# Second MLP products of the next-to-last rows, moved ahead of the last rows' transposes, in a two-layer transformer kernel

## The chip, the core and the metric

The kernel runs on one core of a Trainium2 chip. The metric is the device time of one execution in microseconds (us). A core has a matrix engine (TensorE, in the profile PE for products and PEld for weight loads), a vector engine (VectorE, DVE), an activation engine (ScalarE, ACT), GpSimd (POOL) and a queue engine (SyncE, SP) that issues transfers. PE writes only into PSUM, which has eight banks of 512 float32 per partition; DVE and ACT read sums out of it. Every engine works through its own list of instructions in order, and an instruction may wait on a semaphore that another engine raises.

## The reference

Two identical layers over x of 2048 rows and 512 columns in bfloat16:

```
x = x + A(layernorm(x))     # 32-head attention of width 16, softmax, then @ wo
x = x + B(layernorm(x))     # relu(. @ w1) @ w2, inner width 1792
x = x + A(layernorm(x))
x = x + B(layernorm(x))
```

The layernorm has no learned scale. What matters here is the very end of the second layer: attention's output projection, the residual sum, the norm, and the two MLP products of the last rows.

## The kernel before

The kernel unrolls everything into five instruction lists. A planner written in the kernel decides the order while the program is built: it keeps estimated clocks for the engines, holds groups of PE work in two lists (`urgent` and `work`), and lets `fill_pe`, `fill_v` and `run_dve` place them between the softmax pieces. A group's sum in PSUM is taken out ("evacuated") by a function that `put_evac` (L428) appends to the list `evac`. None of the planner's tables or costs is touched by the change, and up to the end stage the lists of all engines are the same instruction by instruction.

The second layer's rows are cut into chunks. The last two chunks hold one tile of 128 rows each: chunk 5 (the "former rows", tile 14, called `half_tt`) and chunk 6 (the "last rows", tile 15, called `tt`). For a tile of rows the first MLP product has 14 slices `ht[ft]` of 128 inner columns (`NF` = 14), each 4 products with w1; the second product adds up 14 products with w2. In the buffers' names of the order below, two slices lie in one buffer: `ht0` holds slices 0 and 1, `ht5` holds 10 and 11, `ht6` holds 12 and 13. `xx7` holds the rows of both tiles, `w1_0` to `w1_3` and `ktp0_0` onwards hold w1, `wo` the output projection, `ident` an identity matrix: a product with it copies rows into a sum.

After the softmax loop comes an end stage written out by hand (L2491 to L2637), with these steps:

- The last rows' residual and four products with `wo` are summed into bank `banks[0]`, which is bank 0 of the PSUM tile `ps_s1`. The sum misses one product, that of `ot_last`, which DVE still has to normalise (L1308, L1312, L1314).
- `spare_work` (L2534) gives PE other work while it would wait. It takes first whole groups of the planner's lists, here what is left of the former rows' first MLP product (L733 in the profile, evacuated at L1078 by ACT), and then, by `half_part`, the second MLP products of the former rows: a product of the rows with `ident` and then 14 products of 512 columns, all summed into bank 2 of `ps_s1` (`half_bank`). A condition decides whether `half_part` may run: `if urgent or work or held or half_done[0] == NF` returns. `held` is the list of sums that have been computed and not yet taken out.
- The product with `ot_last` completes the sum. DVE takes statistics straight from PSUM (L2574, L803), ACT computes the root (L806, L811), DVE writes the normalised rows `xn` (L821), and ACT copies the sum into `x_t[tt]` (L2579).
- PE transposes `xn` (L2587), and DVE and ACT copy one half each into `xnT` (L2592).
- A loop over `ft` (14 slices and `LOOK` = 3 steps more) computes the last rows' first product and, three steps later, their second, in two halves of 256 columns in two banks. Relu is done by DVE and ACT in turn (L2620, L2618). Both halves begin with a product that puts the residual in, before the loop. At step `LOOK - 1` the rest of the former rows' `half_part` runs. At step 7 the former rows are copied out and stored (L2608).
- ACT and DVE copy the two halves and two queues store them (L2636, L2637).

PE's products of the end stage all stand under L2511, the helper `add`.

Of the kernel before, what the change touches and what calls it, by code (L numbers as in the profile page):

```python
# [26 lines left out]
def kernel(  # L27
# [10 lines left out]
    nc = tc.nc  # L38
# [9 lines left out]
    NF = DFF // P  # L48
# [71 lines left out]
    LAZY = 2  # L120
    HASTE = 12
    LOOK = 3
    NORM_UNITS, DIRECT_UNITS = 10.0, 3.0

    ctx.enter_context(tc.manual_schedule())
    persist = ctx.enter_context(tc.tile_pool(name="persist", bufs=1))
# [299 lines left out]
        return g  # L426

    def put_evac(cost, fn):  # L428
        evac.append((cost, now_pe[0] + PE_TO_DVE, fn, now_bank[0]))

    def left():
# [15 lines left out]
    def start_group(g):  # L447
        (urgent if g in urgent else work).remove(g)
        n = next_bank()
        if n is None:  # L450
            run_dve(0.0, musts)
            n = next_bank(True)
        now_bank[0] = n
        turn[0] += 1
        owner[n] = "filler"
        ready = max(at(g["deps"], "pe"), bank_free[now_bank[0]] + DVE_TO_PE)
        if g["grid"] and not ending[0]:
            n = len(g["grid"]["mms"])
            grid[0] = dict(
                g["grid"], b=bank(), ready=ready, cols=[deque(range(n)) for _ in range(4)],  # L460
                begun=[False] * 4,
            )
            cur.extend((1.0, grid_unit, ready if n == 0 else 0.0, "f") for n in range(n))
            return
        cur.extend(
            (c, fn, ready if n == 0 else 0.0, g["kind"]) for n, (c, fn) in enumerate(g["pieces"])
        )
# [63 lines left out]
        return worst  # L531

    turn = [0]

    def fill_pe(limit, floor=0.0, most=99):

# [1992 lines left out]

    held = []  # L2530

    of_group = [None]

    def spare_work(units):  # L2534

        while units > 0:
            if not cur:
                g = next(
                    (g for q in (urgent, work) for g in q if at(g["deps"], "pe") is not None), None
                )  # L2540
                if g is None:
                    if urgent or work or held or half_done[0] == NF:
                        return units
                    half_part()
                    units -= 1
                    continue
                start_group(g)
                of_group[0] = g["makes"][0][0]
            units -= cur[0][0]
            do_piece()  # L2550
            if not cur:
                if of_group[0] == "h":
                    do_evac()
                else:
                    held.extend(evac)
                    evac.clear()
        return 0
# [4 lines left out]
            add(banks[i], ot[T][:, part(i)], wo[:, T, :], False, False)  # L2562
    ending[0] = True
    bank_no[0] = 0
    held.extend(evac)
    evac.clear()
    spare_work(DIRECT_UNITS)
    for i in rows:
# [7 lines left out]
    ln_root(tag, n_rows)  # L2576
    for i in rows:
        uses(ln_apply(tag, tt + i, i, at_bank(banks[i])), banks[i], "x")
        uses(nc.scalar.copy(out=x_t[tt + i][:], in_=at_bank(banks[i])), banks[i], "x")  # L2579
    spare_work(NORM_UNITS)  # L2580
    for i in rows:
        for n, copy in enumerate((nc.vector.tensor_copy, nc.scalar.copy)):
# [7 lines left out]
                )  # L2590
            of = pt[:, 0 : NDC * P].rearrange("p (c f) -> p c f", c=NDC)[:, cs.start : cs.stop]
            uses(copy(out=xnT[NQS - 1][:, cs.start : cs.stop, part(i)], in_=of), more[n], "xnT")  # L2592
    spare_work(sum(c for c, *_ in cur))
    evac.extend(held)
    held.clear()
    while evac:
# [3 lines left out]
    ending[0], wide[0] = False, True  # L2600

    halves = [(banks[0], slice(0, D // 2)), (banks[1], slice(D // 2, D))]
    for b, cols in halves:
        add(b, ident[:], x_t[tt][:, cols], True, False, "x")
    for ft in range(NF + LOOK):
        if ft == NF // 2:
            for b, x, row in outs:
# [16 lines left out]
            uses(out, b, "h")  # L2624
        while ft == LOOK - 1 and half_done[0] < NF:
            half_part()
        if ft >= LOOK:
            for b, cols in halves:
                add(
                    b, ht[ft - LOOK][:, part(0)], w2[:, ft - LOOK, cols],  # L2630
                    False, ft == NF + LOOK - 1, "h",
                )
# [35 lines left out]
```

## Time and profile before

| | us |
|---|---|
| median of three runs | 1348.62 (1348.41 to 1348.75) |
| the profiled execution | 1350.76 |
| its span, first to last instruction | 1348.8 |
| busy: PE, ACT, DVE, POOL | 1315.8, 1322.1, 1246.1, 830.0 |
| granted TensorE clock | 0.999 |

The span is what the page's times count from, and the 2 us between it and the profiled execution's time lie around it. Busy times are shares of a span that has many stages; the end stage fills its last 18 us, from about 1330. In the rows of the timeline the columns are the start in us, the length in us, the engine, the line, the operation, what it writes and reads, the count that one row merges, and in brackets the idle time ahead of it and what ended it. A row that merges several products runs from the first one's start to the last one's end, and since products overlap, the spacing of starts is what a product costs in a stream.

### The profile page before, as it was taken

Reading aid. Unit: us, or ns where it says so; the run is one execution under the profiler, and the core shown is the slowest. Engines: PE = TensorE matmul, PEld = TensorE weight load, DVE = VectorE, ACT = ScalarE, POOL = GpSimd, SP = SyncE. Lnnn points to the kernel's source line nnn. Section 1 sums busy time; section 2 is a strip of 40 time slices with the busy share of each in tenths; the row PEclk is TensorE's granted clock in tenths of the full one; section 3 lists DMA queues with packets and bytes.
Section 4 is the critical chain, followed back from the end, with each engine's and each line's share of the span. In section 5 each row is a group of like instructions: output and inputs, shape, how many; then the busy total and the mean of one; then the engine's idle time right before and its main releaser. Section 6 shows DMA issues by size and latency. Waiting matters only on the chain.

```text
span 1348.8 us, 48019 instructions
## 1 busy us (share of the span) xinstructions
PE 1315.8 (98%) x20284; PEld 459.8 (34%) x20284; DVE 1246.1 (92%) x2185; ACT 1322.1 (98%) x1416; POOL 830.0 (62%) x1342
## 2 busy tenths in 40 slices
PE   9999999999999999999999999999999999999997
PEld 3322222222222222222222222222344444444665
DVE  8999999999999999989899899999999998899885
ACT  8999999999999999999999999999999999999995
POOL 4358876667666676756556666566556556567441
PEclk9999999999999999999999999999999999999999
DMA  5301012211042110421113100103302421332120
GB/s 141 67 15 24 14 42 53 50 34 34 14 112 57 34 43 19 108 56 37 30 29 94 42 13 6 35 11 77 97 28 41 112 39 47 75 78 62 28 55 19
DMA packets 166823, 66.52 MB, mean 49 GB/s; under 512 B 137776, under 2 KB 161776, under 8 KB 166608
## 3 DMA queue, kind: packets, MB, share of 16 engines
q1 hardware_dynamic: 160080, 57.86, 17.6%
q0 software_dynamic: 5568, 5.15, 2.1%
q8 instruction: 158, 2.59, 0.8%
q10 hardware_dynamic: 960, 0.46, 0.1%
q14 instruction: 57, 0.47, 0.1%
HBM read 38.80 MB, written 4.19 MB: 32 GB/s over the span
## 4 chain that ended last, share of the span: by engine, by line
PE 58%; ACT 32%; DVE 7%; issue 2%; DMA 1%; POOL 0%; ACTq 0%; DVEq 0%; POOLq 0%
PE ps_s L2396 20%; ACT e L2419 16%; PE ps_f L1430 9%; PE ps_o L1430 9%; PE ps_f L473 9%; PE ps_o L473 8%; ACT xx L2419 5%; ACT w L2419 3%; DVE words L1779 2%; ACT vaug L2419 2%; ACT ktl L2419 2%; ACT val L2419 1%; ACT wv L2419 1%; ACT ktp L2419 1%; PE ps_s L2511 1%
## 5 line engine op out<-in xcount | busy, mean ns | idle before, releaser
L2419 ACT ACTIVATE e<-ps_s 128x1024 bf16<-128x1024 f32 (+1 forms) x702 | 780.9, 1203 | 5.2 <-PE ps_s L2396 4.0
L1779 DVE TENSOR_SCALAR words<-ps_s 128x512 int16<-128x512 f32 x833 | 553.4, 683 | 43.0 <-PE ps_s L2396 36.8
L1848 POOL INT64_ADD words<-words x561 | 355.7, 642 | 240.9 <-DVE words L1779 210.3
L2396 PE MATMUL ps_s<-q,ktp 32*128 32x512 bf16 (+2 forms) x4069 | 474.5, 331 | 14.4 <-ACT e L2419 5.0
L2396 PEld LDWEIGHTS <-ktp 32*128 32x128 bf16 x4317 | 151.6, 91 | 457.6 <-issue 451.4
L2419 ACT ACTIVATE xx<-ps_s 128x1024 bf16<-128x1024 f32 x216 | 234.4, 1122 | 0.7 <-PE ps_s L2396 0.5
L2396 PE MATMUL ps_s<-q,ktl 32*128 32x256 bf16 (+2 forms) x1349 | 195.0, 288 | 1.7 <-ACT wkq L2419 0.5
L1430 PEld LDWEIGHTS <-vaug 128*32 128x32 bf16 x4580 | 113.3, 95 | 144.0 <-issue 128.5
L1430 PE MATMUL ps_f<-e,vaug 128*32 128x512 bf16 (+2 forms) x785 | 115.1, 351 | 0.5 <-DVE ht L1080 0.4
L1430 PE MATMUL ps_o<-e,vaug 128*32 128x512 bf16 (+2 forms) x897 | 111.6, 326 | 0.3 <-DVE ht L1080 0.3
L1430 PE MATMUL ps_f<-words,vaug 128*32 128x512 bf16 (+1 forms) x597 | 99.8, 370 | 1.0 <-issue 1.0
L2419 ACT ACTIVATE w<-ps_s 128x1024 bf16<-128x1024 f32 x86 | 93.6, 1117 | 1.3 <-PE ps_s L2396 1.3
L1779 DVE TENSOR_SCALAR xx<-ps_s 128x512 int16<-128x512 f32 x130 | 85.9, 680 | 2.3 <-PE ps_s L2396 1.2
L1848 POOL INT64_ADD xx<-words x103 | 65.7, 640 | 34.4 <-DVE words L1779 21.8
L2419 ACT ACTIVATE vaug<-ps_s 128x1024 bf16<-128x1024 f32 x77 | 84.1, 1135 | 0.3
L473 PE MATMUL ps_f<-w,ht 128*32 128x512 bf16 x1008 | 82.9, 383 | 0.6 <-DVE r L1286 0.6
L1430 PE MATMUL ps_f<-words,vscaled 128*32 128x512 bf16 (+2 forms) x466 | 83.3, 345 | 0.0
L1430 PEld LDWEIGHTS <-val 128*32 128x32 bf16 x2372 | 68.6, 96 | 38.1 <-issue 31.7
L2396 PEld LDWEIGHTS <-ktl 32*128 32x128 bf16 x1349 | 61.6, 92 | 57.4 <-issue 56.0
L1430 PE MATMUL ps_o<-words,vscaled 128*32 128x512 bf16 (+2 forms) x548 | 78.2, 312 | 0.0
L1430 PEld LDWEIGHTS <-vscaled 128*32 128x32 bf16 x1562 | 66.6, 96 | 27.5 <-issue 21.2
L1848 POOL INT64_ADD words<-xx x85 | 52.5, 626 | 31.5 <-DVE xx L1779 27.5
(360 smaller groups left out, 2815.7 us busy)
## 6 DMA issues: line engine op xcount, KB each, us to landing
w<-in_B_w_dram SPq DMA_DIRECT2D x144, 128.0 KB
w<-in_B_w_dram SPq DMA_DIRECT2D x35, 256.0 KB
q<-xn SPq DMA_DIRECT2D x36, 64.0 KB
wv<-in_A_wqkv_dram SPq DMA_DIRECT2D x8, 256.0 KB
away<-xx SPq DMA_DIRECT2D x8, 256.0 KB
xx<-away SPq DMA_DIRECT2D x8, 256.0 KB
out_dram<-xx SPq DMA_DIRECT2D x15, 128.0 KB
xx<-in_A_x_dram SPq DMA_DIRECT2D x14, 128.0 KB
```

The source lines that it names most:

```text
L473: nc.tensor.matmul(G["b"][cols], lhsT[:, cols], rhs, start=not G["begun"][g], stop=not G["cols"][g], tile_position=(0, 32 * g), skip_group ...
L1430: nc.tensor.matmul((ps_f, ps_o)[sg["bank"]][32 * g : 32 * g + 32, 0 : sg["w"]], values[:, 4 * sg["T"] + g, 2 * e : 2 * e + 32], rhs, start ...
L1779: first = nc.vector.tensor_scalar(out=words[which][:, half * QS : (half + 1) * QS], in0=src, scalar1=EXP_BIAS, scalar2=THIRD, op0=ALU.add, ...
L1848: ins = nc.gpsimd.int64_add(of(part).bitcast(I64), of("lin").bitcast(I64), by)
L2396: score = nc.tensor.matmul(b[:, a : a + sg["w"]], kt[32 * g : 32 * g + 32, kc : kc + P], q_home(sg["q"])[32 * g : 32 * g + 32, sg["e"], 0 ...
L2419: ex = nc.scalar.activation(out=eb[:, 0 : place[m]], in_=b[:, 0 : place[m]], func=ACTF.Exp, scale=1.0 / (LOG2E * UNIT),)
L2511: uses(nc.tensor.matmul(out, lhsT, rhs, start=first, stop=last), b, needs=needs)
```

## The change

Four things change, all in the end stage.

1. An evacuation is now marked when it belongs to a first MLP product (`h`): `put_evac` notes it in `h_evacs`. Where the end stage begins, the sums that wait in `evac` were all put into `held`; now those of `h` are taken out at once and only the others are held.
2. `half_part` may run as soon as the slice that it multiplies has been made, whether or not anything is held.
3. The copy of the last rows' sum to `x_t[tt]` by ACT stands behind the copies of `xnT`, and the two residual products of 256 columns move from before the loop into step `LOOK - 1`.
4. `spare_work` in the norm may place 11 units in place of 10, and one unit more behind the transposes. One `half_part` counts as one unit.

```diff
-    NORM_UNITS, DIRECT_UNITS = 10.0, 3.0
+    NORM_UNITS, DIRECT_UNITS, TURN_UNITS = 11.0, 3.0, 1.0
...
     def put_evac(cost, fn):
+        if of_group[0] == "h":
+            h_evacs.append(fn)
         evac.append((cost, now_pe[0] + PE_TO_DVE, fn, now_bank[0]))
...
-                    if urgent or work or held or half_done[0] == NF:
+                    if half_done[0] == NF or ("h", l, j - 1, half_done[0]) not in made:
                         return units
                     half_part()
...
-    held.extend(evac)
+    for e in evac:
+        if e[2] in h_evacs:
+            e[2]()
+        else:
+            held.append(e)
     evac.clear()
     spare_work(DIRECT_UNITS)
...
         uses(ln_apply(tag, tt + i, i, at_bank(banks[i])), banks[i], "x")
-        uses(nc.scalar.copy(out=x_t[tt + i][:], in_=at_bank(banks[i])), banks[i], "x")
     spare_work(NORM_UNITS)
...
             uses(copy(out=xnT[NQS - 1][:, cs.start : cs.stop, part(i)], in_=of), more[n], "xnT")
-    spare_work(sum(c for c, *_ in cur))
+        uses(nc.scalar.copy(out=x_t[tt + i][:], in_=at_bank(banks[i])), banks[i], "x")
+    spare_work(sum(c for c, *_ in cur) + TURN_UNITS)
...
-    for b, cols in halves:
-        add(b, ident[:], x_t[tt][:, cols], True, False, "x")
     for ft in range(NF + LOOK):
...
         while ft == LOOK - 1 and half_done[0] < NF:
             half_part()
+        for b, cols in halves if ft == LOOK - 1 else ():
+            add(b, ident[:], x_t[tt][:, cols], True, False, "x")
```

Behind these lines the changed kernel's line numbers are five or six higher. The order of the instructions shows what moves. On PE, at the product that completes the last rows' sum, the order before:

```order
L2511 LDWEIGHTS ot_last_148 [waits DVE_49]
L2511 MATMUL ps_s1_181<-wo_67,ot_last_148 128x512
L2587 LDWEIGHTS xn0_168 [waits DVE_49]
L2587 MATMUL ps_o_182<-ident_63,xn0_168 128x128
L2587 LDWEIGHTS xn0_168
```

and now:

```order
L2516 LDWEIGHTS ident_63
L2516 MATMUL ps_s1_181<-xx7_80,ident_63 128x512
L2516 LDWEIGHTS ht0_137
L2516 MATMUL ps_s1_181<-w2_72,ht0_137 128x512
L2516 LDWEIGHTS ot_last_148 [waits DVE_49]
L2516 MATMUL ps_s1_181<-wo_67,ot_last_148 128x512
L2516 LDWEIGHTS ht0_137
L2516 MATMUL ps_s1_181<-w2_72,ht0_137 128x512
L2516 LDWEIGHTS ht1_138
L2516 MATMUL ps_s1_181<-w2_72,ht1_138 128x512
```

Two of the former rows' products stand ahead of `ot_last` and eleven (slices 1 to 11, `ht0` to `ht5`) between it and the transposes. All thirteen stood in one block behind the last rows' third w1 slice. Also on PE, from the last transpose to the first product with w1, before:

```order
L2587 LDWEIGHTS xn0_168
L2587 MATMUL ps_s0_180<-ident_63,xn0_168 128x128
L2511 LDWEIGHTS ident_63
L2511 MATMUL ps_s1_181<-xx7_80,ident_63 128x256 [waits Activation_49]
L2511 LDWEIGHTS ident_63
L2511 MATMUL ps_s1_181<-xx7_80,ident_63 128x256
L2511 LDWEIGHTS w1_2_70
L2511 MATMUL ps_o_182<-xnT3_136,w1_2_70 128x128 [waits DVE_49]
```

and now:

```order
L2592 LDWEIGHTS xn0_168
L2592 MATMUL ps_s0_180<-ident_63,xn0_168 128x128
L2516 LDWEIGHTS ht6_143 [waits Activation_49]
L2516 MATMUL ps_s1_181<-w2_72,ht6_143 128x512
L2516 LDWEIGHTS w1_2_70
L2516 MATMUL ps_o_182<-xnT3_136,w1_2_70 128x128 [waits DVE_49]
```

The two residual products, which wait for ACT's copy, have left this place and stand behind the third w1 slice together with the last product of the former rows (slice 13); the product of slice 12 stands here. On ACT, around the norm, before:

```order
L1078 ACTIVATE ht6_143<-ps_s0_180 128x2x128 [waits PE_49]
L806 ACTIVATE va_176<-mv0_174,masks_64 128x1 [waits DVE_49]
L811 ACTIVATE ya_177<-va_176 128x1 [waits Activation_49]
L2579 CAST xx7_80<-ps_s1_181 128x512 [waits DMAHW3_49,DVE_49,Pool_49]
L2592 COPY xnT3_136<-ps_s0_180 128x2x128 [waits PE_49]
L1078 ACTIVATE ht5_142<-ps_f_183 128x2x128 [waits DMASW7_49,DMASW6_49]
```

and now:

```order
L1083 ACTIVATE ht5_142<-ps_f_183 128x2x128 [waits DMASW6_49,DMASW7_49,DVE_49,PE_49]
L1083 ACTIVATE ht6_143<-ps_s0_180 128x2x128 [waits PE_49]
L811 ACTIVATE va_176<-mv0_174,masks_64 128x1 [waits DVE_49]
L816 ACTIVATE ya_177<-va_176 128x1 [waits Activation_49]
L2597 COPY xnT3_136<-ps_s0_180 128x2x128 [waits PE_49]
L2598 CAST xx7_80<-ps_s1_181 128x512 [waits DMAHW3_49,DVE_49,Pool_49]
```

The evacuation of `ht5` stands first instead of last, and the copy of the sum behind that of `xnT`. The lists of DVE, POOL and SP are the same but for one wait: DVE's last copy (L2636, now L2642) waited for PE and ACT and now waits for PE alone.

More of the change, by code (lines that the diff above doesn't have):

```diff
@@ L453, in start_group @@
         now_bank[0] = n
+        of_group[0] = g["makes"][0][0]
         turn[0] += 1
@@ L533 @@
     turn = [0]
+    of_group = [None]
+    h_evacs = []
     def fill_pe(limit, floor=0.0, most=99):
@@ L2530 @@
     held = []
-    of_group = [None]
     def spare_work(units):
@@ L2547, in spare_work @@
                 start_group(g)
-                of_group[0] = g["makes"][0][0]
             units -= cur[0][0]
```

## The prediction

> **What bounds the kernel now.** The change touches the end stage alone, so I read the span first, then the end stage by stretches, then the chain of waits, then the timeline between the chain's pieces. The view by stretches gives length, busy time of PE, PEld, DVE, ACT and POOL, granted clock, share of DMA and GB/s:
>
> ```profile
> core 0: us, PE busy (x) PEld busy (x) DVE busy (x) ACT busy (x) POOL busy (x), PEclk, DMA share, GB/s
> ...
> 1332.60:1335.06 2.46, 0.00 (x0) 0.00 (x0) 1.69 (x3) 0.50 (x2) 0.00 (x0) 1.00 0.00 0
> 1335.06:1336.61 1.55, 1.28 (x19) 1.14 (x20) 0.54 (x2) 1.17 (x4) 0.00 (x0) 1.00 0.00 0
> 1336.61:1339.85 3.24, 3.24 (x19) 1.47 (x17) 0.34 (x2) 0.25 (x1) 0.00 (x0) 1.00 0.00 0
> 1339.85:1345.50 5.65, 5.65 (x73) 5.09 (x71) 1.46 (x5) 2.14 (x7) 0.00 (x0) 1.00 0.07 23
> 1345.50:1348.80 3.30, 0.02 (x1) 0.00 (x0) 0.42 (x1) 0.37 (x1) 0.00 (x0) 1.00 0.14 40
> ```
>
> PE is empty for 2.46 us, the norm. Soon after, it is full for 3.24 us with the block of 15 wide products of the former rows, and then for 5.65 us with the last rows. The chain that ended last says who sets the pace (start, length, what):
>
> ```profile
> 1332.19 0.41 PE ps_s L2511
> ...
> 1332.68 0.71 DVE stats L2574
> ...
> 1334.20 0.82 DVE xn L821
> ...
> 1335.09 0.59 ACT xx L2579
> ...
> 1345.56 0.02 DVEq L2636
> ...
> 1345.63 0.42 DVE xx L2636
> ```
>
> From the product with `ot_last` (1332.19) the chain goes through DVE and ACT to `xn`, then through ACT's copy of the sum, and from there PE's own list sets the time until DVE's last copy. So the block of 15 lies on the path, while the pause ahead of it is a wait for DVE and ACT in which PE could work.
>
> **The change part by part.** The rows from the timeline on which the sum rests:
>
> ```profile
> 1331.48 0.61 PE L733 MATMUL ps_s<-xnT,ktp 128*128 128x128 bf16 x8
> 1331.78 0.35 DVE L1314 SCALAR_TENSOR_TENSOR ot_last<-ps_o,masks,u 128x128 bf16<-128x128 f32 x1
> 1332.12 0.38 ACT L1078 ACTIVATE ht<-ps_s 128x256 bf16<-128x256 f32 x1 [2.22 <-PE ps_s L733]
> 1332.18 0.10 PEld L2511 LDWEIGHTS <-ot_last 128*128 128x128 bf16 x1 [0.27 <-DVE ot_last L1314]
> ...
> 1335.06 0.28 PE L2587 MATMUL ps_o<-ident,xn 128*128 128x128 bf16 x2 [2.48 <-DVE xn L821]
> ...
> 1335.19 0.28 PE L2587 MATMUL ps_s<-ident,xn 128*128 128x128 bf16 x2
> ...
> 1335.39 0.29 DVE L2592 COPY xnT<-ps_o 128x256 bf16<-128x256 bf16 x1 [0.38 <-PE ps_o L2587]
> 1335.57 0.38 ACT L2592 COPY xnT<-ps_s 128x256 bf16<-128x256 bf16 x1
> 1335.72 0.38 PE L2511 MATMUL ps_s<-xx,ident 128*128 128x256 bf16 x2 [0.26 <-ACT xx L2579]
> ...
> 1335.83 0.40 ACT L1078 ACTIVATE ht<-ps_f 128x256 bf16<-128x256 f32 x1
> 1335.94 0.39 PE L2511 MATMUL ps_o<-xnT,w 128*128 128x128 bf16 x4
> 1336.16 0.61 PE L2511 MATMUL ps_s<-xnT,w 128*128 128x128 bf16 x8
> 1336.36 0.29 DVE L2620 TENSOR_SCALAR ht<-ps_o 128x128 bf16<-128x128 f32 x1 [0.68 <-PE ps_o L2511]
> ...
> 1336.61 0.38 PE L2511 MATMUL ps_s<-xx,ident 128*128 128x512 bf16 x1
> ...
> 1339.85 0.39 PE L2511 MATMUL ps_s<-xnT,w 128*128 128x128 bf16 x4
> ...
> 1340.07 0.38 PE L2511 MATMUL ps_s<-w,ht 128*128 128x256 bf16 x2
> ```
>
> Prices of a product in a stream: the 15 wide ones run from 1336.61 to 1339.85, 3.24/15 = 0.216 us each. The twelve products with w1 run from 1335.94 to 1336.61, 0.67/12 = 0.056 each. The two of 256 columns run from 1335.72 to 1335.94, 0.11 each.
>
> (a) *Two products ahead of `ot_last`: -0.17.* The last of the eight L733 products ends at 1332.09 and, being 0.22 long without its followers, starts at 1331.87; PE is free at 1331.93. Two wide products fill it until 1331.93 + 0.43 = 1332.36, and `ot_last`, ready at 1332.18, starts there and not at 1332.19. Of 0.43 us 0.26 lies in the wait for DVE, and 0.17 delays the norm. Behind `ot_last` wait DVE's statistics and all of the chain. Bounds: 0 (the records put PE free too late) and 0.43 (nothing of it is hidden); I take 0.17, since the wait of 0.27 is in the row.
>
> (b) *Eleven products in the norm: free.* They start at 1332.36 + 0.22 = 1332.58 and take 11 x 0.216 = 2.38, until 1334.96. The norm's length, 1335.06 - 1332.19 = 2.87, is DVE and ACT work that none of these products feeds or delays, since they add into another bank; the transposes come at 1335.06 + 0.17 = 1335.23, and PE is free 0.27 before. Without this cover they would cost their 2.38. The norm could stretch because DVE reads PSUM while PE writes it: I take 0, as DVE's relu reads sums in 0.29 at 1340.71 too, in the stretch where PE is busy 5.65 of 5.65, and 0.1 as the upper end. The last two of the eleven wait for ACT's evacuation of `ht5`, whose sum was complete before the eight L733 products ended; ACT is idle 2.22 us ahead of 1332.12, so 0.40 us of it is done by about 1332.1, `ht6` follows, and va, not due before 1333.6, finds ACT free.
>
> (c) *Behind the transposes: 0.12 more.* Let T be the first transpose. Before, the w1 products began at T + 0.88, because two residual products waited for ACT's copy of the sum; the third of the twelve began at T + 0.99. Now the product of slice 12 runs from T + 0.24 to T + 0.46 while DVE copies `xnT` (done at T + 0.62), so it is hidden. The first w1 product can start at T + 0.67. The third needs ACT's half of `xnT`: ACT took that copy 0.10 after the transposes' end (1335.47), DVE took its own 0.05 after (1335.34 to 1335.39); with the copy of the sum gone from ahead of it, I put ACT at T + 0.45, done at T + 0.83, and the third product at T + 0.88. That is 0.11 to 0.12 earlier. Bounds: 0 (ACT comes no sooner) to 0.3 (no wait for ACT at all).
>
> (d) *The block shrinks from 15 to one.* Ten products from the third w1 on end at T + 0.88 + 0.56 = T + 1.44, the product of slice 13 at T + 1.65, the two residual ones (ACT's copy is over by about T + 1.3) at T + 1.87, the four of the next w1 slice at T + 2.09. There the first product of the last rows starts; before it was 1340.07 = T + 5.01. Its slice was evacuated within 0.32 of its sum's end (1336.33 to 1336.65), that is by T + 1.5 now. Gain 2.92, which is 13 x 0.216 = 2.81 plus the 0.12 of (c).
>
> (e) *The end: 0.05.* DVE's last copy waited with one instruction for PE and with itself for ACT, now for PE only. The extra step in the chain is the 0.02 at 1345.56 with an issue gap: 0.07 from there to 1345.63. I take 0.05, between 0 and 0.07; DVE's half is stored last (SP, below), so it counts.
>
> ```profile
> 1345.91 0.36 ACTq L2637 DMA_DIRECT2D out_dram<-xx  x1
> 1346.08 0.34 SPq L2637 DMA_DIRECT2D out_dram<-xx  x1
> ```
>
> The sum: 2.92 - 0.17 + 0.05 = **2.80 us**. The span goes from 1348.8 to 1346.0 and the profiled execution from 1350.76 to about 1347.96. The three timed runs have a median 2.14 below that execution, and work in the last 18 us moves them alike: 1348.62 - 2.80 = **1345.8 us**, 0.21% less.
>
> One page of the Trainium skill speaks against this size. "TensorE: Matmul & The Clock Gate", section "Back-to-back issue gap", gives 131 ns per product of 512 columns in a stream beside 216 ns for one alone. By 131 ns the thirteen products would be worth 13 x 0.131 = 1.70, and the sum would be some 1.7. The row decides: here a stream of such products with a weight load each took 0.216.
>
> **The rivals.**
>
> *The small terms fail.* `ot_last` loses the whole 0.43, because weight loads do not run ahead past the one that waits, and ACT brings nothing in (c): 2.81 + 0.05 - 0.43 = 2.43, 1346.2. For it: the two products do stand in front of the waiting load. Against: the row shows 0.27 of wait to lie in.
>
> *The pause holds less.* The products take their full 0.38 to 0.39 each where they now stand, without overlap. With `ot_last` there are 14 ahead of the transposes, 14 x 0.39 = 5.5 from 1331.93 to 1337.4, and the transposes come 2.3 late: 2.92 + 0.05 - 2.3 = 0.7, 1347.9. The weight loads in the block's own stretch speak against it: 15 products in 3.24. A block that is itself cheaper than 0.216 a product, and so worth less when it goes, would end near 1346.9; that is the Trainium skill's rule of above, and since the block's own rows exclude it, it gets 0.01 within this case.
>
> *The evacuation of `ht5` blocks ACT.* It now stands ahead of va and ya and waits for two software transfers. At the latest it is ready at 1335.83, where ACT ran it without waiting; then `ht5` and `ht6` end at 1336.61, va comes 2.98 late, and 2.92 + 0.05 - 2.98 = 0.0: no change, 1348.6. Against: from 1300 on the trace has no packet of the software queue, only
>
> ```profile
> q1 hardware_dynamic: 2524, 0.51, 7.6%
> q8 instruction: 9, 0.15, 1.6%
> q14 instruction: 1, 0.01, 0.1%
> ```
>
> *Slower: the loop falls into lockstep.* The block of 3.24 us gave the first slices' evacuations time. Without it, each of the 14 steps could have to wait for its relu: 0.22 for w1, 0.05 + 0.29 + 0.05 for the relu and its signals, 0.22 for the two products, 0.83 instead of 0.44, so 14 x 0.39 = 5.5 lost and 1348.62 - 2.80 + 5.5 = 1351.3. From 0.20 of wait per step on (2.80/14) it is slower than before. Against: the lead of three steps does not come from the block. A relu in the middle of the loop and the product that uses its slice:
>
> ```profile
> 1340.71 0.29 DVE L2620 TENSOR_SCALAR ht<-ps_o 128x128 bf16<-128x128 f32 x1 [3.61 <-PE ps_o L2511]
> ...
> 1341.84 0.38 PE L2511 MATMUL ps_s<-w,ht 128*128 128x256 bf16 x2
> ```
>
> The slice is ready at 1341.00 and used 0.84 later, and PE is busy for all of that stretch.
>
> **How the numbers follow.** The forecast, with the sum between 2.5 and 3.1, has 0.75; the small terms failing 0.13; the pause holding less 0.05; ACT blocked 0.04; lockstep 0.03. The predicted time is 1345.8; the forecast's own bounds give 1345.5 to 1346.1, a little more for the spread of 0.34 us between the three runs, and the range takes in the second case and some of the third: 1345.3 to 1346.8. About 0.2% (2.70 us) is what a measurement of this kernel can tell from no change, and the sum lies only 0.10 above it: of the forecast's 0.75 I give 0.55 to a gain over 2.70 and 0.20 to one just under. With the second, third and fourth case that makes faster 0.55, the same 0.41, slower 0.04.
>
> **What would show it.** In the changed kernel's timeline: the product with `ot_last` starts at about 1332.36 and the statistics at 1332.85; PE's idle time ahead of the transposes is about 0.3 and not 2.5; the transposes start at 1335.23; three w1 slices follow without a gap from about T + 0.9, and the first pair of the last rows' products starts near 1337.3; SP issues the last store near 1343.3. The prediction is wrong in (a) if `ot_last` starts at 1332.6, in (b) if the transposes start more than 2.9 after `ot_last` or PE has no idle time ahead of them, in (c) and (d) if the last rows' first pair starts later than T + 2.2, in the fourth rival's favour if va starts after 1334, and in the fifth's if steps of the loop are longer than 0.44.

## The result, and the profile after

The changed kernel takes 1345.89 us (median of eight runs, 1344.06 to 1346.81). The kernel before takes 1349.25 (median of eight runs, 1347.17 to 1350.79; the three that the prediction had are among them). The ratio is 0.9973, with a 95% interval of 0.9962 to 0.9984. As a time that is 3.6 us less, and between 2.2 and 5.1.

The forecast was 1345.8 and a gain of 2.80. The changed kernel's time fits; the forecast gain lies in the lower part of the interval. The experiments show that the gain has two parts: 2.72 us in the end stage, which the prediction worked out step by step, and about one us more that it did not know of.

The profiled execution of the changed kernel took 1346.19 us with a span of 1344.4 and a mean granted clock of 1.000. In its program the lines have moved: the helper `add` is L2516 (before L2511), the statistics L2580 (L2574), `xn` L826 (L821), the transposes L2592 (L2587), the copies of `xnT` L2597 (L2592), the copy of the sum L2598 (L2579), the last copies and stores L2642 and L2643 (L2636, L2637). The view by stretches, with the same columns as in the prediction, for the norm, the work from the transposes to the last rows' first pair, the last rows, and the tail:

```profile
1331.07:1333.53 2.46, 2.36 (x11) 0.88 (x9) 1.69 (x3) 0.50 (x2) 0.00 (x0) 1.00 0.00 0
1333.53:1335.40 1.87, 1.80 (x21) 1.34 (x22) 0.82 (x3) 1.14 (x3) 0.00 (x0) 1.00 0.00 0
1335.40:1341.07 5.67, 5.67 (x74) 5.09 (x71) 1.51 (x6) 2.15 (x8) 0.00 (x0) 1.00 0.07 23
1341.07:1344.40 3.33, 0.00 (x1) 0.00 (x0) 0.42 (x1) 0.36 (x1) 0.00 (x0) 1.00 0.14 39
```

The norm is as long as before, and its DVE and ACT work is the same 1.69 and 0.50 us, but PE is busy for 2.36 us of it, where it was empty. The stretch of 3.24 us with nothing but the former rows' products is gone. The last rows take the 5.7 us that they took. The timeline of the changed kernel, from the rows that answer to those in the prediction:

```profile
1329.80 0.61 PE L738 MATMUL ps_s<-xnT,ktp 128*128 128x128 bf16 x8
1330.00 0.38 ACT L1083 ACTIVATE ht<-ps_f 128x256 bf16<-128x256 f32 x1 [1.78 <-PE ps_f L738]
1330.25 0.38 PE L2516 MATMUL ps_s<-xx,ident 128*128 128x512 bf16 x1
1330.46 0.38 PE L2516 MATMUL ps_s<-w,ht 128*128 128x512 bf16 x1
1330.51 0.10 PEld L2516 LDWEIGHTS <-ot_last 128*128 128x128 bf16 x1 [0.16 <-DVE ot_last L1319]
1330.68 0.38 PE L2516 MATMUL ps_s<-wo,ot_last 128*128 128x512 bf16 x1
1330.90 2.54 PE L2516 MATMUL ps_s<-w,ht 128*128 128x512 bf16 x11
1331.17 0.70 DVE L2580 BATCH_NORM_STATS2 stats<-ps_s 128x6 f32<-128x512 f32 x1 [0.71 <-PE ps_s L2516]
...
1332.68 0.81 DVE L826 TENSOR_SCALAR xn<-ps_s,mv,ya 128x512 bf16<-128x512 f32 x1 [0.60 <-ACT ya L816]
...
1333.55 0.29 PE L2592 MATMUL ps_o<-ident,xn 128*128 128x128 bf16 x2
...
1333.98 0.37 ACT L2597 COPY xnT<-ps_s 128x256 bf16<-128x256 bf16 x1 [1.34 <-PE ps_s L2592]
1334.21 0.46 PE L2516 MATMUL ps_o<-xnT,w 128*128 128x128 bf16 x4
...
1334.96 0.38 PE L2516 MATMUL ps_s<-w,ht 128*128 128x512 bf16 x1
1335.18 0.38 PE L2516 MATMUL ps_s<-xx,ident 128*128 128x256 bf16 x2
...
1335.62 0.38 PE L2516 MATMUL ps_s<-w,ht 128*128 128x256 bf16 x2
...
1341.46 0.39 ACTq L2643 DMA_DIRECT2D out_dram<-xx  x1
1341.56 0.34 SPq L2643 DMA_DIRECT2D out_dram<-xx  x1
```

The clock times of the two profiles differ by 1.68 us before the end stage begins (the eight products start at 1329.80, before at 1331.48), where the programs are the same; two profiles of the unchanged kernel before differ by more (1331.48, and 1328.84 in e0_before below). So all comparisons here run from a mark inside the end stage: S, the start of the eight products L738 (before L733); O, the start of the product with `ot_last`; T, the first transpose; F, the first pair of the last rows' second products. The end is the span's.

| us | before | after | forecast of the step |
|---|---|---|---|
| S to O | 0.71 | 0.88 | 0.17 longer |
| O to T | 2.88 | 2.87 | 2.87 |
| T to F | 5.01 | 2.07 | 2.09 |
| F to SP's issue of the last store | 6.01 | 5.94 | 0.05 shorter |
| that issue to the end | 2.73 | 2.85 | the same |
| S to the end | 17.34 | 14.61 | 2.80 shorter |

The stage is shorter by 2.72 us. The chain of waits of the changed kernel:

```profile
1330.41 0.66 PE ps_s L2516 x3
...
1331.17 0.71 DVE stats L2580
...
1332.68 0.82 DVE xn L826
...
1333.87 0.30 DVE xnT L2597
...
1334.21 0.46 PE ps_o L2516 x4
1334.68 1.32 PE ps_s L2516 x17
```

Three products stand in the chain's first piece where one stood, which is the 0.17 that `ot_last` lost. Behind `xn` the chain now goes through DVE's copy of `xnT` and no longer through ACT's copy of the sum. From 1334.21 on PE's own list sets the time again, without the block.

### The profile page after: what moved, and what is told of

Same layout as the page of the kernel before. It is cut to its first block, busy times and chain, and to the rows that moved or that the text cites. A ratio compares the mean times of both kernels' runs of the same rounds, so it can differ in the third digit from the quotient of the medians.

```text
span 1344.4 us, 48018 instructions
## 1 busy us (share of the span) xinstructions
PE 1313.7 (98%) x20283; PEld 461.0 (34%) x20284; DVE 1243.7 (93%) x2185; ACT 1322.1 (98%) x1416; POOL 828.5 (62%) x1342
## 4 chain that ended last, share of the span: by engine, by line
PE 58%; ACT 32%; DVE 6%; issue 2%; DMA 2%; POOL 0%; SPq 0%; DVEq 0%; ACTq 0%; POOLq 0%
PE ps_s L2401 20%; ACT e L2424 16%; PE ps_f L1435 10%; PE ps_o L1435 9%; PE ps_f L476 9%; PE ps_o L476 8%; ACT xx L2424 5%; ACT w L2424 3%; DVE words L1784 2%; ACT ktl L2424 2%; ACT vaug L2424 2%; ACT val L2424 1%; ACT wv L2424 1%; ACT ktp L2424 1%; ACT wkq L2424 1%
```

## The experiments

The theory at this point (A) was that the end stage alone accounts for the gain, by the prediction's own steps. The rival (B) was that something ahead of the end stage, or around it, also differs from kernel to kernel, since 3.6 is more than 2.72. The runs came in three series, each on one chip beside runs of the kernel before. The table gives each kernel's number of runs and their mean time, and then the same for those runs whose mean granted clock, rounded to three places, was 1.000. The runs e5, e6, e7 and e10 have one execution each (1346.50, 1345.42, 1348.16 and 1347.38 us), so from them only the profile is used.

| | runs | mean us | with a mean clock of 1.000 | their mean us |
|---|---|---|---|---|
| first series: before | 25 | 1349.22 | 8 | 1348.18 |
| e0_before | 11 | 1350.21 | 3 | 1348.08 |
| e1_after | 6 | 1345.06 | 6 | 1345.06 |
| e2_no_fill | 12 | 1349.75 | 2 | 1347.60 |
| e3_best | 6 | 1345.16 | 5 | 1344.87 |
| second series: before | 17 | 1350.31 | 4 | 1349.12 |
| e4_dummy | 12 | 1348.19 | 11 | 1348.10 |
| third series: before | 19 | 1349.94 | 4 | 1348.34 |
| e8_after | 8 | 1346.16 | 6 | 1345.60 |
| e9_best | 5 | 1345.23 | 4 | 1344.89 |
| e11_dummy4 | 12 | 1349.53 | 5 | 1348.25 |

### The two kernels again: e0_before, e1_after, e8_after

No edit: the kernel before with a new profile, and the changed kernel on two further chips.

> The kernel before, against itself, for the spread. In the profiled executions the end stage went from 17.33 us (from the first of the eight L733 products into ps_s to the end of the span) to 14.61, 2.72 less, but the spans went from 1348.8 to 1344.4, 4.4 less, so 1.7 us came from ahead of the change; the first profile has one stretch of 3.4 us (637.3 to 640.7) with the clock at half. Theory A (the rest is chance, a window of half clock that comes and goes, and all that the change does is in the end stage): this run differs from before by no more than 1.5 us either way, the end stage takes 17.3 again, and a profile without such a stretch has a span near 1347. Theory B (something ahead of the end stage was systematically slower in the kernel before): every profile of this kernel has some 1.7 us more ahead of the end stage than the changed one.

> The changed kernel once more. Theory A: end stage 14.6 us (2.7 to 2.8 less than before), time 2.3 to 3.3 us under the kernel before. Theory B: 3.4 us or more under it again, and ahead of the end stage at least 1 us less.

> The changed kernel on one chip beside the version that uses more of the pause. Pause theory: end stage 14.61 to 14.64 us in the profile, as twice before, clock 1.0 in most executions, and the time 2.8 us under those executions of the kernel before that had clock 1.0, some 4 us under its mean.

The ratios to the kernel before are 1.0008 (0.9998 to 1.0018) for e0_before, 0.9973 (0.9961 to 0.9984) for e1_after and 0.9972 (0.9962 to 0.9983) for e8_after. So the result stands in each series. On the means e1_after is 4.2 us under the kernel before, which is what theory B expected of it. The stage repeats too: S to the end is 14.64 and 14.63 in the two new profiles of the changed kernel. But the new profile of the kernel before does not repeat the old one. Its T to F is 6.67 us and not 5.01, and S to the end 19.00 and not 17.34. Its view by stretches:

```profile
1329.90:1332.40 2.50, 0.04 (x1) 0.00 (x0) 1.69 (x3) 0.50 (x2) 0.00 (x0) 1.00 0.00 0
1332.40:1333.50 1.10, 0.81 (x10) 0.67 (x11) 0.29 (x1) 1.05 (x3) 0.00 (x0) 1.00 0.00 0
1333.50:1337.00 3.50, 3.50 (x19) 1.85 (x17) 0.58 (x2) 0.38 (x2) 0.00 (x0) 0.51 0.00 0
1337.00:1340.50 3.50, 3.50 (x33) 2.37 (x32) 0.29 (x1) 0.59 (x3) 0.00 (x0) 1.00 0.00 0
```

The granted clock is 0.51 in the third row. The trace shows the borders: from 1333.53 to 1336.95, for 3.41 us, the clock is half and the products start at twice their usual distance, and then at the usual one again. The timeline of e0_before inside that stretch:

```profile
1335.21 0.15 PEld L2511 LDWEIGHTS <-ht 128*128 128x128 bf16 x1 [0.28 <-issue]
1335.64 0.15 PEld L2511 LDWEIGHTS <-ht 128*128 128x128 bf16 x1 [0.28 <-issue]
```

The weight loads of two wide products follow each other at 0.43 us, which is 2 x 0.216. PE was full all the while, so half of the 3.41 us, 1.7, is lost on the path: 6.67 - 5.01 = 1.66. The stretch begins 1.1 us behind the end of the norm's pause of 2.5 us. The clock of the profile that the prediction used was 1.00 in every stretch of the end stage; that execution had no such stretch there. It has one at 637 us, and so have e2 and e10; this one is not tied to the change.

S is reached at 1328.84 in e0_before, 1328.13 in e1_after and 1329.95 in e8_after (1331.48, with the stretch at 637 us, and 1329.80 in the two first profiles): what lies ahead of the end stage is not longer in the one kernel than in the other. So theory B falls in the form "ahead of the end stage", and a new one takes its place (C): the empty pause brings on the half clock in part of the executions, and the changed kernel, which has no empty pause, is spared it.

### Parts 1 and 3 without the filling: e2_no_fill

```diff
-    NORM_UNITS, DIRECT_UNITS, TURN_UNITS = 11.0, 3.0, 1.0
+    NORM_UNITS, DIRECT_UNITS, TURN_UNITS = 0.0, 2.25, 0.0
```

Sums are still taken out at once and the residual still comes later, but no product of the former rows stands ahead of `ot_last`, in the norm or behind the transposes.

> The changed kernel without any of the former rows' products in the pause (none ahead of ot_last, none in the norm, none behind the transposes): all 15 stand in the block again. The early evacuation, the late copy of the sum and the late residual products stay. Pause theory (the gain is products moved into a wait): the time is that of the kernel before or up to 0.2 us more, since the residual products of 0.22 us now lie in the full stretch; from the first transpose to the last rows' first pair 5.1 us (5.01 before, 2.07 in the changed kernel). Order theory (the gain comes from the copy and the residual being out of the way, or from the sums taken out early): most of the 2.8 us stays.

The ratio is 1.0005 (0.9996 to 1.0013): without the products in the pause nothing is gained. Its view by stretches shows the half clock in the end stage again, in the third row, from 1337.64 on, 1.75 us behind the pause:

```profile
1333.40:1335.85 2.45, 0.01 (x1) 0.00 (x0) 1.69 (x3) 0.50 (x2) 0.00 (x0) 1.00 0.00 0
1335.85:1337.60 1.75, 1.44 (x18) 1.16 (x19) 0.68 (x3) 1.14 (x3) 0.00 (x0) 1.00 0.00 0
1337.60:1341.00 3.40, 3.40 (x10) 1.20 (x9) 0.20 (x1) 0.00 (x0) 0.00 (x0) 0.51 0.00 0
```

T to F is 6.78 here, and 5.09 in the two profiles below that keep the same order without a half clock. The 5.09 are 0.08 to 0.09 more than before: part 3 puts the two residual products into the stretch where PE is full, and they no longer lie in the wait for `xnT`.

### A full pause that saves nothing: e4_dummy and e11_dummy4

This separates theory C from theory A. The products of the former rows stay where they were before, and the pause is filled with eleven products whose sums are overwritten (in e11 with four):

```diff
+    NORM_UNITS, DIRECT_UNITS, TURN_UNITS = 0.0, 2.25, 0.0
...
-    spare_work(NORM_UNITS)
+    for ft in range(11):
+        add(half_bank, ht[ft % 10][:, half_at : half_at + P], w2[:, ft, :], True, True, "none")
```

> The kernel without the fill (the block of 15 stays behind the third w1 slice) and with eleven products in the norm's pause whose sum is thrown away: they write into the former rows' bank, which the block's first product then starts afresh. The output is the reference's. In the kernel before and in the one without fill, one execution each showed TensorE's clock at half for 3.4 us from 1.1 us behind the pause, which made the stretch from the first transpose to the last rows' first pair 6.7 to 6.8 us in place of 5.0 to 5.1. Clock theory (the pause now and then brings on a window of half clock, and work in the pause prevents it): no such window at the end, that stretch is 5.1 us, the lowest times stay at those without fill (1347.5), but the mean comes down from 1349.9 by 0.5 to 1.5 us, and most executions show a mean clock of 0.999 or more. Chance theory (the window has nothing to do with the pause): the spread and the mean stay, 1349 to 1350.5, with mean clocks of 0.997 in some.

> As the run with eleven thrown-away products, but with four, right behind ot_last, so that PE's empty stretch ahead of the transposes is 2.0 us (2.88 - 0.86 counted by starts, 1.6 without a product in flight) instead of 2.88 (2.5). If the window of half clock needs most of a 3.4 us window to be empty, four products are enough: mean near 1348.2 and clock 1.0 in most executions, as with eleven. If any pause above 1.5 us can bring it on, the mean stays near that without fill (1349.7) and clocks of 0.997 to 0.999 are common.

With eleven the ratio is 0.9985 (0.9977 to 0.9994), which is 2.0 us less (0.8 to 3.1), though its end stage, 17.42 us, is none the shorter. Of its 12 runs 11 have a mean clock of 1.000, against 4 of 17 of the kernel before on the same chip and 2 of 12 for e2 on the chip of the first series. The clock need not be all of the 2.0: the four runs of the kernel before with a mean of 1.000 still lie 1.0 above those of e4, though four runs that spread from 1346.96 to 1351.70 don't settle that. Its view by stretches has the full pause in the first row, and in the third, where the block stands, the full clock:

```profile
1330.50:1333.00 2.50, 2.40 (x12) 0.88 (x9) 1.69 (x3) 0.50 (x2) 0.00 (x0) 1.00 0.00 0
1333.00:1334.40 1.40, 1.11 (x16) 0.96 (x17) 0.51 (x2) 0.86 (x2) 0.00 (x0) 1.00 0.00 0
1334.40:1338.00 3.60, 3.60 (x24) 1.81 (x21) 0.37 (x2) 0.28 (x1) 0.00 (x0) 1.00 0.00 0
```

With four products, which leave PE empty for 1.62 us of the pause, the ratio is 0.9996 (0.9988 to 1.0005), and 5 of 12 runs have the full clock. Its timeline around the pause:

```profile
1329.64 1.03 PE L2516 MATMUL ps_s<-w,ht 128*128 128x512 bf16 x4
...
1332.29 0.28 PE L2593 MATMUL ps_o<-ident,xn 128*128 128x128 bf16 x2 [1.62 <-DVE xn L826]
```

So this shorter pause is not seen to help. Where its seven other runs lost their clock stays open, since its one profile has no half clock in the end stage while PE has work.

Over all profiles the picture is this: with the empty pause the half clock stood in the end stage, while PE had work, in two of three (e0, e2, not in before), with the pause full in none of ten. One such stretch lowers the mean clock of an execution to 0.999 (0.5 x 3.41/1349 = 0.0013), so an execution with a mean of 1.000 had none. The reverse does not hold. The stretches at 637 us count too, and so does a half clock after PE's last product, which costs nothing: the 0.999 of e7 comes from its last 1.36 us alone. What lowered the mean of four of the changed kernel's 22 runs was not traced.

The traces also show why only some executions are hit. The clock changes only at borders that lie whole multiples of 3.413 us apart; in e0_before it changes at 5.75, 1333.53, 1336.95 and 1347.19, in steps of 389, 1 and 3 such windows. PE's busy time in single windows, first the one right ahead of the half clock in e0_before and in e2_no_fill, then the two that the pause falls into in the profile of the kernel before that the prediction used:

```profile
1330.12:1333.53 3.41, 0.84 (x11) 0.70 (x12) 1.91 (x4) 1.58 (x5) 0.00 (x0) 1.00 0.00 0
...
1334.23:1337.64 3.41, 1.48 (x18) 1.19 (x19) 1.71 (x5) 1.64 (x5) 0.00 (x0) 1.00 0.00 0
...
1330.20:1333.62 3.42, 2.28 (x31) 1.11 (x19) 2.48 (x6) 0.38 (x1) 0.18 (x1) 1.00 0.02 5
1333.62:1337.03 3.41, 1.71 (x20) 1.34 (x21) 1.61 (x4) 1.92 (x6) 0.00 (x0) 1.00 0.00 0
```

In the last two rows a border at 1333.62 cuts the pause into two parts, and the clock stays full. Over all windows of the 14 profiles, counted from the first change to full clock, half clock followed each of the eleven in which PE was busy for 1.48 us or less (nine of them at the very end, where PE runs out of work), and none in which it was busy for 1.66 or more, except those ahead of the three stretches at 637 us (2.54 us busy), whose cause stays open. So what counts is not the length of the pause but how much of one window it empties, and that depends on where the borders fall. If they fall anywhere with equal chance, then by an estimate from PE's busy time in e0_before the empty pause leaves a window with at most 1.48 us of work in 0.70 of the executions, and one with at most 1.66 in 0.81. Of the kernel before, 53 of 72 executions had a mean clock under 1.000, those with a stretch at 637 us included. In the changed kernel and with eleven products thrown away, no placing of a window in the end stage, while PE still has work to come, leaves under 3.0 us of work. With four products thrown away the emptiest placing holds 1.52, between the two figures, so the rows do not say which way that kernel goes.

The Trainium skill, "TensorE: Matmul & The Clock Gate", section "What's actually happening", describes a half-rate clock and an activity window of 3413 ns that runs freely. The length agrees with the 3.41 us here, and a window that runs freely would fit that only a part of the executions is hit. The table in the page's section "Why this matters for your kernels" advises against idle gaps of more than about 3 us. Here a gap of 2.5 us was enough, in a PE that is otherwise busy for 98% of the span, wherever it left one window with 1.48 us of work or less. The measurement decides.

### The early evacuation undone: e5_held

```diff
-    for e in evac:
-        if e[2] in h_evacs:
-            e[2]()
-        else:
-            held.append(e)
+    held.extend(evac)
```

together with noting the group's name only where `spare_work` starts it, as before. (The loop alone has no effect here: without it the program is the same. What takes the sum out early is that a group begun before the end stage is now known as `h` by name.)

> The changed kernel with the early evacuation undone alone (the sum of ht5 is again put by when its group ends, and taken out where it was before). Pause theory: slices 10 to 13 cannot be multiplied in the pause, nine products follow ot_last, PE idles 0.9 us ahead of the transposes instead of 0.5, four products stand in the block, and the last rows' first pair comes at T + 2.7 to T + 2.95 instead of T + 2.07 (two to four products of 0.216, and up to 0.2 for ht5's evacuation, then late on ACT): 0.65 to 0.9 us of the gain belong to this part. Rival (the slices would have been taken anyway): T + 2.1.

In its profile T to F is 2.95 and not 2.07, S to the end 15.53 and not 14.61. Its timeline behind the transposes:

```profile
1333.97 0.40 ACT L1082 ACTIVATE ht<-ps_f 128x256 bf16<-128x256 f32 x1
...
1334.43 0.54 PEld L2515 LDWEIGHTS <-ht 128*128 128x128 bf16 x4 [0.23 <-ACT ht L1082]
1334.43 1.04 PE L2515 MATMUL ps_s<-w,ht 128*128 128x512 bf16 x4
```

Four products of 512 columns are left behind the transposes in place of one (3 x 0.216 = 0.65), and PE waits 0.23 for the evacuation of `ht5`, which again comes late: 0.88 together. So the early evacuation is worth 0.9 of the 2.7.

### The residual back at its old place: e6_residual_first

```diff
     uses(ln_apply(tag, tt + i, i, at_bank(banks[i])), banks[i], "x")
+    uses(nc.scalar.copy(out=x_t[tt + i][:], in_=at_bank(banks[i])), banks[i], "x")
...
+    for b, cols in halves:
+        add(b, ident[:], x_t[tt][:, cols], True, False, "x")
     for ft in range(NF + LOOK):
```

> The changed kernel with its third part undone alone: ACT's copy of the sum stands ahead of the copies of xnT again, and both residual products ahead of the loop. By the terms as I summed them this part is worth 0.12 us behind the transposes and 0.05 at the end. By a recount with all products in their places: the residual products then lie in the wait for xnT, where they cost nothing, and not in the full stretch, so T to the first pair is 1.98 instead of 2.07 us, and only the end loses 0.07: a wash. If the late copy is what matters: T + 2.2 or more.

In its profile T to F is 1.98 and not 2.07, so part 3 alone costs 0.09, as in e2. SP's issue of the last store comes at S + 11.74 (11.76 in the changed kernel), and the end at S + 14.47 (14.61 to 14.64). So part 3 earns nothing, and by this one profile it costs 0.14: what it wins in the wait for ACT's half of `xnT` (0.13) it more than gives back with the two residual products in the full stretch (0.22), and what it wins at DVE's last copy (0.07) it loses again at the stores (0.12).

The end differs by more than the issue, and the last stores differ too. The timeline of e6 at its end:

```profile
1340.72 0.36 ACTq L2643 DMA_DIRECT2D out_dram<-xx  x1
1340.89 0.34 SPq L2643 DMA_DIRECT2D out_dram<-xx  x1
```

The two issues lie 0.17 apart, in the changed kernel 0.10 (1341.46 and 1341.56 above), where ACT's issue also takes 0.39 and not 0.36. In all six profiles with the shorter distance (after, e1, e5, e7, e8, e10) the end follows SP's issue by 2.85 to 2.89 us; in the eight with 0.16 to 0.17 (before, e0, e2, e3, e4, e6, e9, e11) by 2.71 to 2.73. So in these profiles bringing SP's store closer to ACT's did not pay. The cause was not tried.

### How many products ahead of `ot_last`, and in the norm: e7_four_ahead, e10_overfill

```diff
-    NORM_UNITS, DIRECT_UNITS, TURN_UNITS = 11.0, 3.0, 1.0
+    NORM_UNITS, DIRECT_UNITS, TURN_UNITS = 11.0, 4.5, 1.0      (e7)
+    NORM_UNITS, DIRECT_UNITS, TURN_UNITS = 14.0, 2.25, 1.0     (e10)
```

In e7 four products stand ahead of `ot_last` in place of two; in e10 none does, and all fifteen stand in the norm.

> Four of the former rows' products ahead of ot_last instead of two, all the others behind it in the pause, none left for later. Pause theory: ot_last starts 0.43 us later (1.31 us after the first of the eight products, 0.88 in the changed kernel), the norm keeps its 2.87 us, the first pair comes at T + 1.85 (one product less on the path), and from the first of the eight to the last store it is 0.21 us more than the changed kernel. Rival (weight loads ahead of a waiting one hide it, or the norm runs faster or slower beside a full PE): ot_last less than 0.3 later, or T - O other than 2.87 by over 0.1.

> All of the former rows' 15 products in the norm's pause, none ahead of ot_last and none behind. Pause theory: ot_last starts 0.71 us after the first of the eight, 15 x 0.216 = 3.24 us of products follow it at once and hold the transposes until 3.46 us after ot_last instead of 2.87; the first pair comes at T + 1.86, and from the first of the eight to the last store it takes 12.0 us, 0.2 more than the changed kernel: past 2.65 us of work (2.87 less ot_last's 0.22) the pause is full and each product costs its 0.216. Rival (the norm itself stretches or products in the pause are cheaper): T - O of less than 3.3 or more than 3.6.

e7: S to O is 1.310 and not 0.878. Two more products cost 0.432 = 2 x 0.216, nothing of it hidden, as expected once the wait is used up. SP's issue comes 0.22 later than in the changed kernel, since one product of 0.216 fewer stands behind the transposes. e10: O to T is 3.464 and not 2.87, and T to F 1.84. The timeline of e10 around the norm:

```profile
1331.90 3.19 PE L2516 MATMUL ps_s<-w,ht 128*128 128x512 bf16 x14
...
1333.47 0.81 DVE L826 TENSOR_SCALAR xn<-ps_s,mv,ya 128x512 bf16<-128x512 f32 x1 [0.60 <-ACT ya L816]
1334.71 0.42 PEld L2592 LDWEIGHTS <-xn 128*128 128x128 bf16 x4
```

`xn` is ready at 1334.28, but the transposes' weights load at 1334.71 and the transposes start 0.64 behind `xn`, since PE still works on the fifteen. The pause holds twelve and no more. The three that are too many cost 0.59 there. Against the changed kernel, 0.17 of that comes back at `ot_last`, which starts in time, and 0.23 from T to F, so that SP's issue comes 0.20 later after S.

### The version that the runs point to: e3_best, e9_best

One product ahead of `ot_last`, the copy of the rows with `ident`, which needs nothing from DVE or ACT; twelve in the norm; two behind the transposes. The left half of the last rows' second product is added straight onto the residual sum, which lies in that bank already, so that one product with `ident` and half of ACT's copy fall away. The main lines of the edit (ACT's copy is also cut to its right half, and `half_part` no longer begins with the copy of the rows):

```diff
+    NORM_UNITS, DIRECT_UNITS, TURN_UNITS = 12.0, 2.25, 2.0
...
     spare_work(DIRECT_UNITS)
+    add(half_bank, ident[:], x_t[half_tt][:], True, False, "none")
...
-        for b, cols in halves if ft == LOOK - 1 else ():
+        for b, cols in halves[1:] if ft == LOOK - 1 else ():
```

> A version that uses what is left: only the product with ident (0.22 us) ahead of ot_last, 12 slices in the norm, the last two behind the transposes, and the first half of the last rows' second product added straight onto the sum with the residual, so that one residual product and half of ACT's copy fall away. Pause theory: ot_last starts as early as before (0.71 us after the first of the eight L738 products, 0.88 in the changed kernel), the transposes follow 2.87 us later with PE free 0.07 us ahead of them, the first pair at T + 1.75 instead of T + 2.07; together 0.49 us less than the changed kernel, 3.3 less than before. Rival (the pause is full already): the transposes wait for the twelfth slice and the gain over the changed kernel is under 0.2 us.

> The version of run e3_best again, to set it against the changed kernel on the same chip. Pause theory: end stage 14.0 us, 0.6 less than the changed kernel (0.49 from PE's list, 0.1 from the two last stores, which are issued 0.16 us apart and not 0.105), so the mean of its executions with clock 1.0 is 0.4 to 0.8 us below that of the changed kernel. Rival (what differs from execution to execution ahead of the end stage hides it): no difference that can be told.

The two new profiles agree: S to the end is 14.008 in both, 0.6 less than in the changed kernel. The timeline of e3_best:

```profile
1329.55 0.38 PE L2516 MATMUL ps_s<-xx,ident 128*128 128x512 bf16 x1
...
1329.81 0.10 PEld L2516 LDWEIGHTS <-ot_last 128*128 128x128 bf16 x1 [0.22 <-DVE ot_last L1319]
...
1330.05 2.75 PE L2516 MATMUL ps_s<-w,ht 128*128 128x512 bf16 x12
...
1332.93 0.59 PE L2516 MATMUL ps_s<-w,ht 128*128 128x512 bf16 x2
```

`ot_last` starts 0.71 after S, as before the change (0.17 won); the two products at 1332.93 lie in the wait for `xnT`; from T to F it takes 1.745 and not 2.07 (0.216 for the product and 0.11 for the one with `ident`); and the stores are 0.16 apart again (0.12). The ratios to the kernel before are 0.9972 (0.9961 to 0.9983) and 0.9965 (0.9953 to 0.9977). It beats the kernel before; by time it can't be told apart from the changed kernel (means of 1345.16 against 1345.06 in the first series, 1345.23 against 1346.16 in the third; among runs with a mean clock of 1.000 it is 0.2 and 0.7 less, where 0.4 to 0.8 was expected). That it is 0.6 us better rests on the profiles.

## Why the prediction was right, and what it missed

*(a) Two products ahead of `ot_last`: right.* S to O grew by 0.17, as forecast; e7 shows that beyond the wait each further product costs its whole 0.216, and e3 that one product is free.

*(b) Eleven products in the norm: right.* O to T is 2.87, as before. The statistics take 0.70 and `xn` 0.81 with PE full (0.71 and 0.82 in the chain before), so DVE reading PSUM was not slowed. The last of the eleven starts 0.49 ahead of T, and the start of the next could have come 0.28 ahead: 0.27 was forecast. e10 sets the limit: it is passed at the point that 0.216 per product gives.

*(c) and (d): the sum right, its parts named wrongly.* The third product with w1 started at T + 0.86 (forecast 0.88), F at T + 2.07 (2.09), and the gain is 2.94 (2.92). But "13 x 0.216 plus 0.12" is not how it came about. Fourteen products left the full stretch (3.02), two residual ones of 0.11 came into it (-0.22), where before they had stood in the wait for `xnT`, and the third product with w1 came 0.13 earlier: 3.02 - 0.22 + 0.13 = 2.93. The right total came of following each product to its place; the wording hid that part 3 earns nothing (0.13 - 0.22), which e6 shows.

*(e) The end: wrong in sign, by 0.10.* DVE's copy came 0.07 sooner, as the row of the extra step suggested, and SP's issue too. But the end followed the issue 0.12 later, so that 0.05 was lost where 0.05 was to be won. The step took a store's time from issue to end as fixed.

The stage thus gained 2.72 where 2.80 was forecast. At a mean clock of 1.000 the runs agree: 1345.06 against 1348.18 in the first series, 1345.60 against 1348.34 in the third, 3.1 and 2.7 less.

*What was missed: the pause also costs clock.* The prediction took the pause for a time in which PE could have worked and costed it at no more. In part of the executions it also halves the clock for 3.41 us of full PE work behind it, 1.67 us on the path. On the means the whole gain is 4.2 and 3.8 us in the two series against 2.72 in the stage, so 1.1 to 1.4 are left for the clock. At 1.67 us in 0.70 to 0.81 of the executions the estimate from the windows is 1.2 to 1.4 at most. The stretches at 637 us are in the means too, and their share was not measured. That the predicted time came out right is in part luck: it was drawn from a median of three runs, 1348.62, that lay 0.6 below the one of all eight (1349.25), and the gain was short by about as much. The bound that failed is "work in the last 18 us moves them alike", by which the gain of one execution was carried to the median of others.

*The rivals.* "The small terms fail" falls: (a) and (c) held, and (e) was off by no more than 0.10. "The pause holds less" falls: eleven products took 2.54 from the first start to the last end. "The evacuation of `ht5` blocks ACT" falls: that evacuation ran at 1330.00, and va was not held up (the norm has its length). "The loop falls into lockstep" falls: the steps of the loop stay at 0.44, and PE is busy for 5.67 of 5.67 in the last rows. The mechanism of e4, a gain by the clock alone, was not among the rivals, so the chance of 0.41 for a gain within 0.2% took no account of it. (Of the cases as they are listed, 0.42 and 0.03 follow for the same and for slower, not 0.41 and 0.04.)

## What to carry to other kernels

A pause of the matrix engine on the path costs twice: the work that could have stood there, and, where it is some 2.5 us long in a dense stream, the clock of the next 3.4 us in part of the executions: in those where it leaves under some 1.5 us of work in one of the windows of 3.41 us that the traces show. One profile can miss this, so the granted clock should be read over several executions. Filling such a pause with work that is on the path later is worth the work's spacing in a stream, up to the point where the last product still ends before the awaited one can begin; count for every product both the stretch that it leaves and the one that it enters. Moving a step out of a wait into a full stretch gives back what it wins.

## What the hardware showed that was not expected

- The clock fell to half (0.51 granted) for 3.41 us after a pause of 2.5 us in a PE busy for 98% of the span: in two of three profiles with the empty pause, in none of ten with the full one. It followed windows of 3.41 us with 0.84 and 1.48 us of PE work, and did not follow those with 1.66 or more (but for 637 us). Of runs with a mean clock of 1.000 there were 19 of 72 for the kernel before, 18 of 22 for the changed one, 11 of 12 for eleven products thrown away, 5 of 12 for four.
- Two stores of 64 KB from two queues, issued 0.10 us apart, ended 2.85 to 2.89 after the second issue; issued 0.16 to 0.17 apart, 2.71 to 2.73.
- A bank that PE fills did not slow DVE's reads from another: 0.70 and 0.81 us for the statistics and `xn`, with PE busy for 2.36 of 2.46 us and with PE empty.
